# Moving VectorE and GpSimd pieces apart in a hand-ordered gated-attention and feed-forward kernel

## The chip, the cores and the metric

One core of a Trainium2 chip. The metric is the device time of one execution in microseconds, as the median of several runs of the slowest core (there is only one here). TensorE is called PE below, VectorE DVE, ScalarE ACT, GpSimd POOL, and the queue that issues most transfers SP.

## What is computed

A gated linear attention over 768 steps for 32 heads of width 48, whose output goes through a feed-forward layer:

```python
f = 1.0 / (1.0 + np.exp(-f_logit))            # q, k, v, f_logit: (4, 8, 768, 48), fp32
for t in range(S):
    state = f[:, :, t, :, None] * state + np.einsum('bhd,bhe->bhde', k[:, :, t], v[:, :, t])
    y[:, :, t] = np.einsum('bhd,bhde->bhe', q[:, :, t], state)
x = y.transpose(0, 2, 1, 3).reshape(B * S, H * D)      # (3072, 384)
h = x @ w_in                                           # w_in (384, 2048)
g = 0.5 * (h + np.sqrt(h * h + 4.0))
out = g @ w_out                                        # w_out (2048, 384)
```

## The kernel before

The 3072 rows are cut into 12 pairs of two chunks (256 steps each, three pairs to a batch entry). Within a chunk the recurrence is done as matrix products: with the running sum of log f inside the chunk, q is scaled by its negative exponential, k by the positive one, a masked product of q and k gives the part from inside the chunk, and a carried state gives the rest.

The whole kernel is a list of *pieces*. `describe` (L125) defines each piece by name with the engines that may run it; `ORDER` is one long string that lists all 1032 pieces as `name:engine`, with PSUM banks behind `@` for those that take one, and with `TABLE:e` and `TABLE:s` where ACT loads the table for exponentials and logarithms or the one for square roots (six of each). The loop at L567 walks the string and emits piece after piece. Each engine runs its own pieces in the order of the string, and a piece waits until what it reads is there and the buffer that it writes is free. So the string sets everything: the engine of a piece, its place in that engine's queue, and what stands behind it when it waits.

The pieces of pair p, with the lines that the trace shows (L137 and L140 are the helpers for copies and products, so their rows are told apart by the tiles):

- `lf, lq, lk, lv` load f_logit, q, k, v (SP). `wi0` to `wi3` and `wo0` to `wo7` load the weights w_in and w_out in blocks, issued by POOL (L146, L151).
- `ex`, `ln` (ACT, L180, L188) make s, the negative log of f. `ad` adds the two rows of a partition into ss (L194). `hi` and `lo` split ss into two fp16 halves in the tile hl (cast L137, subtraction L203), `cu` sums them along the chunk on PE (L211, L217), `c1` subtracts (L225, tile cm), `ea` and `ep` are the exponentials (ACT, L236), `ge` another small one (L259), `gs` and `gb` small products of it.
- `qm`, `km` make the scaled q and k in the tile qk (products L140, inputs q and ea or k and ep), two each per pair. `vc` casts v to fp16 (tile v16, L137). `tp`, `te` (pairs 0 to 3, PE and copies) or `tx` (pairs 4 to 11, transposing transfers on SP) transpose qk into qkT.
- `sc` (PE, L319), `pm` (DVE, L327, applies the mask while reading PSUM), `kv` (PE, L338), `yt` (PE, L388), `yn` (PE, L397), `sp`, `sa`, `sb` (state update, tiles st and sn), `yc` (copy of y). `xp`, `xe` or `xx` transpose y into xT.
- `m1.p.m` (PE, L436, six matmuls), `sq` (ACT, L445, the square, tile hsq), `rt` (ACT, L450, the root, tile r16, one for two squares), `gt` (DVE, L460, g from PSUM and r), `m2` (PE, L472, four matmuls), `ev` (copy of the output), `st` (store, L493).

Pieces `ad, hi, lo, gs, gb, qm, km, vc`, and `sa, sb` where the state comes from st, read SBUF alone. They may run on DVE or POOL (`hi` and `vc` also on ACT). `pm, gt, c1, sp` and the copies out of PSUM read PSUM and can't run on POOL. `r16` has three buffers: a root waits until the `gt` pieces of three roots earlier have read theirs.

Of the kernel before, what the change touches and what calls it, by code (L numbers as in the profile page):

```python
# [30 lines left out]
tp0.1:T@23 te0.0.0:D te0.1.0:A hi2.0:P te0.0.1:D te0.1.1:A lk2.0:S wi0:P lo2.0:D ea1.00:A sc0.1:T@45 ea1.01:A km1.01:P
sc0.0:T@67 ep1.00:A pm0.11:D lv1.0:S vc0.0:A cu2.0:T@0 pm0.00:D vc0.1:A qm1.01:P pm0.01:D kv0:T@23 ep2.01:A lq2.0:S wi2:P
pm0.10:D ea2.01:A ex3.0:A sa0:D yt0:T@56 km1.00:P c12.0:D ge2:A yn0.1:T ea2.00:A yc0.0:D qm1.00:P ia0.1:T lf5.0:S ep2.00:A
yc0.1:D xp0.0:T@7 ge1:A gb1:P xp0.1:T@4 xe0.0:A wi1:P tp1.0:T@20 ln3.0:A xe0.1:D ex4.0:A ad3.0:D m1.0.1:T@5 te1.1.0:D ln4.0:A
m1.0.0:T@1 te1.0.0:D sq0.1:A ad4.0:P sb0:D sc1.1:T@67 sq0.0:A sc1.0:T@40 pm1.11:D TABLE:s gs2:P lv2.0:S hi3.0:P m1.0.5:T@2
pm1.01:D lo3.0:P pm1.10:D m1.0.4:T@3 rt0.0:A pm1.00:D wi3:P cu3.0:T@7 sq0.5:A gt0.0:D gs1:P sq0.4:A km2.00:P gt0.1:D
m1.0.3:T@0 rt0.2:A c13.0:D km2.01:P lq3.0:S m1.0.2:T@6 sq0.3:A vc1.0:D sq0.2:A gt0.5:D kv1:T@41 lk3.0:S ia1.0:T rt0.1:A
gt0.4:D yt1:T@52 qm2.00:P sa1:D yn1.0:T TABLE:e yc1.0:D qm2.01:P gt0.2:D xp1.0:T@3 yn1.1:T ia1.1:T xe1.0:D ea3.00:A gb2:P
yc1.1:D tp2.0:T@45 wo1:P ep3.00:A sb1:D ep3.01:A xp1.1:T@6 wo3:P lf6.0:S m1.0.6:T@3 te2.1.0:D ea3.01:A ge3:A ex5.0:A
m1.0.7:T@2 te2.0.0:D wo0:P xe1.1:D sq0.6:A sc2.0:T@17 wo2:P lv3.0:S gt0.3:D sc2.1:T@54 ln5.0:A m1.1.3:T@6 pm2.00:D vc2.0:P  # L40
# [5 lines left out]
ep5.01:A c15.0:D m2.0.02:T ep4.01:A c14.0:D ep5.00:A m2.0.12:T gt1.6:D ge5:A ge4:A ex6.0:A lq4.0:S m2.0.03:T vc3.0:P ea4.01:A
m2.1.03:T ep4.00:A ev0.0:D lv4.0:S ea4.00:A xp2.1:T@4 gs4:D xp2.0:T@0 ev1.0:D ln6.0:A tp3.0:T@32 xe2.1:D gb4:D kv3:T@15
xe2.0:D ex7.0:A ad6.0:P lk5.0:S m1.2.3:T@4 sa3:D ea5.01:A te3.0.0:D m1.2.2:T@0 ln7.0:A km4.00:P te3.1.0:D m2.0.13:T lf8.0:S
ea5.00:A ad7.0:P sp3.1:D sq2.3:A sc3.1:T@17 ev0.1:D sc3.0:T@32 sq2.2:A m1.2.0:T@5 km4.01:P pm3.00:D TABLE:s lf9.0:S
m1.2.1:T@6 pm3.10:D qm4.00:P pm3.01:D m2.1.10:T@3 rt2.1:A hi6.0:D m1.2.5:T@1 vc4.0:P sq2.0:A m1.2.4:T@2 gt2.2:D sq2.1:A  # L50
gt2.3:D m2.1.11:T sq2.4:A pm3.11:D km5.00:P m1.2.7:T@0 rt2.0:A qm4.01:D m1.2.6:T@4 km5.01:P sq2.5:A gt2.0:D tx4.0:S m2.1.12:T
rt2.2:A gb5:D lo6.0:P gt2.1:D m2.1.13:T sq2.6:A m2.2.10:T@7 gt2.4:D hi7.0:P tx4.1:S ev1.1:A qm5.01:P gt2.5:D yt3:T@56 sq2.7:A
kv4:T@23 sb3:D rt2.3:A qm5.00:P yn3.1:T yc3.0:D m2.2.00:T@1 yc3.1:D TABLE:e m2.2.01:T lo7.0:P tx5.0:S sp4.0:D cu6.0:T@5
gt2.7:D sa4:P m2.2.11:T ex9.0:A gt2.6:D xp3.0:T@6 tx5.1:S xp3.1:T@2 ep6.01:A cu7.0:T@0 xe3.1:D ex8.0:A xe3.0:D m2.2.02:T
sp4.1:D ge7:A ea7.01:A c16.0:D sc4.1:T@42 ep7.01:A lv5.0:S sc4.0:T@63 pm4.10:D ge6:A ep6.00:A m2.2.03:T lk7.0:S ln8.0:A
pm4.01:D m1.3.0:T@4 lq7.0:S c17.0:D ea6.00:A lk6.0:S m2.2.12:T ad8.0:P pm4.00:D ep7.00:A m2.2.13:T ea6.01:A ev2.0:D sb4:P
ea7.00:A pm4.11:D sc5.0:T@30 ln9.0:A sc5.1:T@65 hi8.0:P pm5.00:D m1.3.1:T@1 gs5:P sq3.0:A vc5.0:P ev2.1:D yt4:T@23 sq3.1:A
pm5.01:D lo8.0:P yn4.0:T TABLE:s m1.3.5:T@7 pm5.11:D ad9.0:P yn4.1:T yc4.0:D m1.3.7:T@0 yc4.1:D rt3.0:A m1.3.4:T@5 qm7.01:P
pm5.10:D xx4:S sq3.5:A kv5:T@23 gt3.0:D km7.00:P yt5:T@63 sq3.4:A gt3.1:D yn5.0:T sq3.7:A lf10.0:S m1.3.3:T@4 sp5.0:D
km6.01:P rt3.2:A lv7.0:S m1.3.2:T@1 sa5:D lq6.0:S hi9.0:P yc5.0:D m1.3.6:T@2 sq3.3:A lv6.0:S km6.00:P gt3.5:D sq3.2:A yn5.1:T  # L60
# [550 lines left out]
```

## Time and profile before

| | |
|---|---|
| median of 3 runs | 199.15 us (198.51 to 201.0) |
| the profiled execution, its own time | 198.22 us |
| its span in the trace | 196.3 us |
| PE busy (matmul) | 169.8 us, 86% |
| ACT busy | 162.3 us, 83% |
| DVE busy | 155.2 us, 79% |
| POOL busy | 86.7 us, 44% |

Busy time is what the trace books between start and end of an instruction; an instruction that waits for something after it has started counts as busy. A row of a timeline gives start, length, engine, line, operation, the tiles written and read, how many instructions are merged in it, and in brackets the idle time of the engine ahead of it with what ended it. Consecutive instructions of an engine overlap by up to a tenth of a microsecond, so starts are a better measure of a step than lengths.

### The profile page before, as it was taken

The page shows a single profiled execution, that of the slowest core. Times are in us where ns is not written, and L with a number is a line of the kernel's source. Part 1 is how long each engine was busy: PE and PEld are TensorE (multiplying, and loading weights), DVE is VectorE, ACT ScalarE, POOL GpSimd, SP SyncE. Part 2 cuts the span into 40 slices and gives each one's busy share as a digit, 9 for nine tenths or more (in the row PEclk, how much of TensorE's full clock was granted, in tenths as well). Part 3 has the DMA queues.
Part 4 walks back from the last instruction along what each step waited for, and adds up shares of the span by engine and source line. Part 5 has one row for each costly group of instructions (what it writes and reads, how often), then busy time and mean ns, then how long its engine had stood idle before and what let it go on. Part 6 is the DMA issues. An engine that isn't in the chain of part 4 may idle for free.

```text
span 196.3 us, 5562 instructions
## 1 busy us (share of the span) xinstructions
PE 169.8 (86%) x2279; PEld 123.3 (63%) x2279; DVE 155.2 (79%) x285; ACT 162.3 (83%) x268; POOL 86.7 (44%) x117
## 2 busy tenths in 40 slices
PE   0248976998699999979999999999999899999990
PEld 0125654785367676867577776677867767767650
DVE  4489779999979999994999959879687559456450
...
GB/s 138 275 261 249 248 251 267 240 217 224 242 135 80 16 136 173 244 183 294 129 227 129 243 292 168 230 146 90 219 170 102 147 80 3 85 106 14 80 83 82
DMA packets 80538, 32.88 MB, mean 167 GB/s; under 512 B 73888, under 2 KB 80496, under 8 KB 80512
## 3 DMA queue, kind: packets, MB, share of 16 engines
...
q0 software_dynamic: 3824, 3.24, 10.3%
...
## 4 chain that ended last, share of the span: by engine, by line
issue 30%; ACT 25%; DVE 20%; PE 15%; DMA 4%; POOL 3%; SPq 1%; POOLq 0%; DVEq 0%; ACTq 0%
DVE g L460 7%; ACT r L450 6%; PE ps L436 6%; ACT hsq L445 4%; DVE pm L327 3%; PE ps L472 3%; ACT ep L236 3%; ACT ea L236 3%; ACT f L180 2%; ACT s L188 2%; DMA q<-in_q_dram 2%; ACT L571 2%; DVE v L137 2%; DMA f<-in_f_logit_dram 1%; POOL sn L140 1%
## 5 line engine op out<-in xcount | busy, mean ns | idle before, releaser
L460 DVE SCALAR_TENSOR_TENSOR g<-ps,r 128x512 f16<-128x512 f32 x96 | 62.2, 684 | 18.7 <-ACT r L450 18.2
L436 PE MATMUL ps<-xT,win 128*128 128x256 f16 x576 | 71.9, 276 | 3.3 <-DMA win<-in_moe_w_in_dram 1.1
L472 PE MATMUL ps<-wout,g 128*128 128x384 f16 x384 | 70.5, 326 | 0.3 <-DVE g L460 0.2
L436 PEld LDWEIGHTS <-win 128*128 128x128 f16 x576 | 55.3, 99 | 14.1 <-DMA xT<-y 2.8
L445 ACT ACTIVATE hsq<-ps 128x512 f16<-128x512 f32 x96 | 54.1, 601 | 11.9 <-PE ps L436 11.6
L450 ACT ACTIVATE r<-hsq 128x1024 f16<-128x1024 f16 x48 | 50.5, 1063 | 4.2 <-DVE g L460 3.4
L472 PEld LDWEIGHTS <-g 128*128 128x128 f16 x384 | 35.9, 98 | 20.8 <-DVE g L460 1.4
L327 DVE TENSOR_TENSOR pm<-ps,mask 128x512 f16<-128x512 f32 x48 | 30.5, 684 | 1.5 <-PE ps L319 1.5
L140 POOL TENSOR_TENSOR qk<-q,ea 128x384 f16<-128x384 f32 (+1 forms) x19 | 18.4, 978 | 13.8 <-DMA q<-in_q_dram 12.6
L140 POOL TENSOR_TENSOR qk<-k,ep 128x384 f16<-128x384 f32 (+1 forms) x20 | 20.1, 1012 | 4.4 <-DMA k<-in_k_dram 4.3
L211 PE MATMUL ps<-hl,tri 128*128 128x384 f16 (+1 forms) x26 | 7.3, 355 | 13.0 <-DVE hl L137 6.3
L194 POOL TENSOR_TENSOR ss<-s 128x384 f32<-128x384 f32 x8 | 8.1, 1009 | 18.2 <-ACT s L188 18.2
L140 POOL TENSOR_TENSOR sn<-st,gs 128x384 f16<-128x384 f32 x5 | 4.1, 829 | 25.4 <-DVE st L364 25.4
L137 DVE CAST y<-ps 128x384 f16<-128x384 f32 x20 | 10.8, 550 | 3.0 <-PE ps L397 2.9
L180 ACT ACTIVATE f<-f 128x768 f32<-128x768 f32 (+1 forms) x13 | 10.3, 795 | 2.6 <-DMA f<-in_f_logit_dram 2.5
L211 PEld LDWEIGHTS <-tri 128*128 128x128 f16 x26 | 2.4, 102 | 14.0 <-issue 7.1
L493 POOL DMA_DIRECT2D out_dram<-os x1 | 0.6, 604 | 22.8 <-DVE os L137 22.8
L188 ACT ACTIVATE s<-f 128x768 f32<-128x768 f32 (+1 forms) x13 | 10.5, 807 | 0.2
L140 DVE TENSOR_TENSOR qk<-q,ea 128x384 f16<-128x384 f32 (+1 forms) x7 | 9.2, 1312 | 1.7 <-issue 1.5
L319 PE MATMUL ps<-qkT 48*64 48x128 f16 x384 | 9.0, 229 | 1.2 <-DVE qkT L137 0.5
L319 PEld LDWEIGHTS <-qkT 48*64 48x64 f16 x384 | 6.4, 112 | 4.9 <-issue 2.8
L137 POOL CAST v<-v 128x768 f16<-128x768 f32 x9 | 8.2, 913 | 2.6 <-PE ps L436 1.5
...
## 6 DMA issues: line engine op xcount, KB each, us to landing
...
```

Of the source, the lines that this page charges most:

```text
L137: eng(e).tensor_copy(out=o, in_=i)
L140: eng(e).tensor_tensor(out=o, in0=a, in1=b, op=ALU.mult)
L180: nc.scalar.activation(out=t, in_=t, func=AF.Exp, scale=-1.0)
L188: nc.scalar.activation(out=T["s", p][:, :, hs], in_=T["f", p][:, hs].rearrange("p h i d -> p i h d"), func=AF.Ln, bias=1.0)
L236: nc.scalar.activation(out=T[nm, p][:, i, hs].rearrange("p h d -> p (h d)"), in_=src_, func=AF.Exp, scale=sgn)
L319: nc.tensor.matmul(out=T["sc", p, i, h][64 * cc:64 * cc + 64, j, :], lhsT=t[r, 1, j, i, :], rhs=t[r, 0, j], start=True, stop=True)
L327: eng(e).tensor_tensor(out=T["pm", p, i, h], in0=T["sc", p, i, h], in1=K["mask"][:, i].unsqueeze(1).broadcast_to([128, 4, 128]), op=ALU.mult)
L436: nc.tensor.matmul(out=T["h", p, m][:, a], lhsT=K["win"][m // 2][:, j, m % 2 * 256 + a * 128:m % 2 * 256 + a * 128 + 128], rhs=T["xT", p][ ...
L445: nc.scalar.activation(out=T["hsq", p, r][:, a], in_=T["h", p, m].rearrange("p a c t -> p (a c t)"), func=AF.Square, scale=1.0)
L450: nc.scalar.activation(out=T["r16", p, r], in_=T["hsq", p, r], func=AF.Sqrt, scale=0.25, bias=1.0)
L460: nc.vector.scalar_tensor_tensor(out=T["g", p][:, 2 * m:2 * m + 2, :].rearrange("p a t -> p (a t)"), in0=T["h", p, m].rearrange("p a c t - ...
L472: nc.tensor.matmul(out=T["o", p, cc], lhsT=T["g", p][:, jn, cc * 128:(cc + 1) * 128], rhs=K["wout"][jn // 2][:, jn % 2, :], start=(jn == 0 ...
```

## The change

Only the string `ORDER` changes. It holds the same 1032 pieces, with the same code, buffers and depths. They stand in another order, many have other PSUM banks, and 70 have another engine: 29 go from DVE to POOL, 20 from POOL to DVE, one from POOL to ACT, nine from DVE to ACT, ten from ACT to DVE, one store from SP to POOL. The pieces that read SBUF alone with two inputs or for a cast were 42 on DVE and 92 on POOL and are 34 and 100.

The diff replaces the string from its first line to its last. One line of each, around the end of pair 1's first layer:

```diff
 ORDER = """
...
-m2.0.10:T@6 rt1.0:A qm3.00:D qm3.01:P m2.0.01:T rt1.2:A gt1.1:D m1.1.7:T@0 lo4.0:P gs3:D lo5.0:D m2.0.11:T sq1.6:A gt1.0:D
...
+rt1.0:A wo6:P m2.0.10:T@3 sq1.4:A gt1.1:D qm3.01:P m2.0.00:T@6 sq1.6:A gt1.0:D m2.0.01:T rt1.2:A km3.01:P m2.0.11:T sq1.7:A
...
```

Four places, as the instructions stand in the built programs. A name is tile, underscore, buffer. The first is DVE from the last y copies of pair 2 to the g of pair 1 (g_962 before, g_960 after); y16 is the y copy, ss the sum, gs a small product, hl the split sum, qk the scaled q and k, ps a PSUM bank. Before:

```order
L137 CAST y16_937<-ps4_885 128x384
L194 TENSOR_TENSOR ss_943<-s_810 128x384
L137 CAST y16_937<-ps1_884 128x384
L460 SCALAR_TENSOR_TENSOR g_962<-ps6_812,r16_939 128x512
L460 SCALAR_TENSOR_TENSOR g_962<-ps0_824,r16_939 128x512
L140 TENSOR_TENSOR qk0_95<-q_596,ea_692 128x4x2x48
L460 SCALAR_TENSOR_TENSOR g_962<-ps7_861,r16_980 128x512
L140 TENSOR_TENSOR gs_999<-ge_754,half_87 128x24
L203 TENSOR_TENSOR hl1_92<-ss_943,hl1_92 128x8x48
L460 SCALAR_TENSOR_TENSOR g_962<-ps5_872,r16_980 128x512
L460 SCALAR_TENSOR_TENSOR g_962<-ps2_945,r16_988 128x512
L460 SCALAR_TENSOR_TENSOR g_962<-ps4_955,r16_988 128x512
```

After:

```order
L137 CAST y16_943<-ps2_889 128x384
L137 CAST y16_943<-ps7_888 128x384
L460 SCALAR_TENSOR_TENSOR g_960<-ps3_873,r16_945 128x512
L460 SCALAR_TENSOR_TENSOR g_960<-ps6_824,r16_945 128x512
L460 SCALAR_TENSOR_TENSOR g_960<-ps1_862,r16_980 128x512
L460 SCALAR_TENSOR_TENSOR g_960<-ps4_813,r16_980 128x512
L460 SCALAR_TENSOR_TENSOR g_960<-ps5_949,r16_1003 128x512
L460 SCALAR_TENSOR_TENSOR g_960<-ps0_936,r16_1003 128x512
```

The ss sum of pair 5, a q product of pair 3, a gs and the subtraction of pair 5 no longer stand between these g; the two y copies and the six g are the same.

The second is POOL in the same stretch, from the eighth block of w_out on (wout7) to the cast of v of pair 3 (v16). Before:

```order
L137 CAST hl1_92<-ss_943 128x8x48
L151 DMA wout7_120<-in_moe_w_out_dram 128x2x384
L151 DMA wout6_119<-in_moe_w_out_dram 128x2x384
L140 TENSOR_TENSOR qk0_95<-q_596,ea_692 128x4x2x48
L203 TENSOR_TENSOR hl0_91<-ss_491,hl0_91 128x8x48
L140 TENSOR_TENSOR qk0_95<-k_629,ep_732 128x4x2x48
L137 CAST v16_1084<-v_789 128x768
```

After:

```order
L151 DMA wout7_120<-in_moe_w_out_dram 128x2x384
L194 TENSOR_TENSOR ss_922<-s_822 128x384
L137 CAST hl1_92<-ss_922 128x8x48
L140 TENSOR_TENSOR qk0_95<-k_668,ep_728 128x4x2x48
L203 TENSOR_TENSOR hl1_92<-ss_922,hl1_92 128x8x48
L151 DMA wout6_119<-in_moe_w_out_dram 128x2x384
L140 TENSOR_TENSOR qk0_95<-q_604,ea_691 128x4x2x48
L140 TENSOR_TENSOR qk0_95<-k_668,ep_728 128x4x2x48
L140 TENSOR_TENSOR qk0_95<-q_604,ea_691 128x4x2x48
L137 CAST v16_1130<-v_835 128x768
```

POOL now makes the ss sum and the subtraction of pair 5 and all four products of pair 3 (tile qk0); the subtraction for pair 4 (hl0_91) has gone to DVE, and the seventh block of w_out (wout6) stands behind four pieces, three of which POOL did not have before.

The third is POOL near the start, from the ss sum of pair 2 to the third issue of w_in (win0, win2, win1 in this order). Before:

```order
L194 TENSOR_TENSOR ss_239<-s_206 128x384
L137 CAST hl0_91<-ss_239 128x8x48
L146 DMA win0_109<-in_moe_w_in_dram 128x3x512
L140 TENSOR_TENSOR qk1_96<-k_149,ep_237 128x4x2x48
L140 TENSOR_TENSOR qk1_96<-q_179,ea_268 128x4x2x48
L146 DMA win2_111<-in_moe_w_in_dram 128x3x512
L140 TENSOR_TENSOR qk1_96<-k_149,ep_237 128x4x2x48
L140 TENSOR_TENSOR qk1_96<-q_179,ea_268 128x4x2x48
L140 TENSOR_TENSOR gb_420<-gs_208,ge_418 128x8
L146 DMA win1_110<-in_moe_w_in_dram 128x3x512
```

After:

```order
L194 TENSOR_TENSOR ss_253<-s_211 128x384
L146 DMA win0_109<-in_moe_w_in_dram 128x3x512
L203 TENSOR_TENSOR hl0_91<-ss_253,hl0_91 128x8x48
L146 DMA win2_111<-in_moe_w_in_dram 128x3x512
L146 DMA win1_110<-in_moe_w_in_dram 128x3x512
L140 TENSOR_TENSOR qk1_96<-k_171,ep_287 128x4x2x48
```

The cast of pair 2 between the ss sum and win0 is gone to DVE; one subtraction (hl0_91) stands between win0 and win2, and win1 follows win2 directly, ahead of the products of pair 1 (qk1), three of which DVE now makes.

The fourth is DVE among the g of pair 2 (g_1330) after the change; ss_1361 belongs to pair 7 and qk2_97 to pair 5:

```order
L460 SCALAR_TENSOR_TENSOR g_1330<-ps7_1211,r16_1299 128x512
L137 CAST y16_1326<-ps5_1266 128x384
L460 SCALAR_TENSOR_TENSOR g_1330<-ps6_1201,r16_1299 128x512
L194 TENSOR_TENSOR ss_1361<-s_1103 128x384
L140 TENSOR_TENSOR qk2_97<-q_1136,ea_1197 128x4x2x48
L460 SCALAR_TENSOR_TENSOR g_1330<-ps1_1319,r16_1352 128x512
L460 SCALAR_TENSOR_TENSOR g_1330<-ps4_1224,r16_1352 128x512
```

The ss sum and the q product are new on DVE there; before, POOL made both.

## Rows read from the trace of the kernel before

**Rows 1.** The page, part 1: busy us, share of span, instructions.

```profile
PE 169.8 (86%) x2279; PEld 123.3 (63%) x2279; DVE 155.2 (79%) x285; ACT 162.3 (83%) x268; POOL 86.7 (44%) x117
```

**Rows 2.** Busy us by stretch; at the end granted clock, DMA share, GB/s.

```profile
22.00:52.00 30.00, 23.87 (x384) 17.73 (x385) 28.32 (x44) 24.93 (x38) 18.92 (x26) 1.00 1.19 242
...
60.00:120.00 60.00, 58.50 (x789) 42.84 (x788) 54.16 (x97) 58.39 (x95) 38.83 (x46) 1.00 0.99 183
120.00:190.00 70.00, 68.47 (x848) 50.34 (x845) 49.55 (x85) 55.76 (x89) 13.51 (x17) 1.00 0.56 110
```

**Rows 3.** DVE by shape: line, operation, tiles, count | busy us, mean ns.

```profile
L140 DVE TENSOR_TENSOR qk<-q,ea 128x384 f16<-128x384 f32 x5 | 8.1, 1617 | 1.5 <-issue 1.5
...
L137 DVE CAST v<-v 128x768 f16<-128x768 f32 x2 | 3.3, 1631 | 0.0
...
L140 DVE TENSOR_TENSOR qk<-k,ep 128x384 f16<-128x384 f32 x3 | 2.1, 686 | 0.0
```

**Rows 4.** Timeline of DVE: start us, length us, line, operation, tiles.

```profile
22.80 0.56 DVE L194 TENSOR_TENSOR ss<-s 128x384 f32<-128x384 f32 x1 [0.43 <-ACT s L188]
...
45.44 4.55 DVE L140 TENSOR_TENSOR qk<-q,ea 128x384 f16<-128x384 f32 x1
49.92 0.68 DVE L460 SCALAR_TENSOR_TENSOR g<-ps,r 128x512 f16<-128x512 f32 x1
...
52.87 0.54 DVE L140 TENSOR_TENSOR qk<-k,ep 128x384 f16<-128x384 f32 x1
```

**Rows 5.** Timeline of POOL beside the long DVE product.

```profile
45.99 1.01 POOL L140 TENSOR_TENSOR qk<-q,ea 128x384 f16<-128x384 f32 x1
46.96 0.91 POOL L203 TENSOR_TENSOR hl<-ss,hl 128x384 f16<-128x384 f32 x1
47.83 0.99 POOL L140 TENSOR_TENSOR qk<-k,ep 128x384 f16<-128x384 f32 x1
48.77 0.81 POOL L137 CAST v<-v 128x768 f16<-128x768 f32 x1
```

**Rows 6.** Timeline of ACT: the root that waited for g.

```profile
51.85 1.06 ACT L450 ACTIVATE r<-hsq 128x1024 f16<-128x1024 f16 x1 [3.41 <-DVE g L460]
```

**Rows 7.** Timeline of PE between 22 and 52 us.

```profile
22.88 2.74 PE L436 MATMUL ps<-xT,win 128*128 128x256 f16 x12
...
29.53 1.48 PE L436 MATMUL ps<-xT,win 128*128 128x256 f16 x12 [1.11 <-DMA win<-in_moe_w_in_dram]
32.42 0.52 PE L338 MATMUL ps<-v,qk 64*128 64x96 f16 x16 [1.41 <-DVE v L137]
...
50.66 0.34 PE L211 MATMUL ps<-hl,tri 128*128 128x384 f16 x1 [2.46 <-DVE g L460]
```

**Rows 8.** Timeline of POOL: first and third issue of w_in.

```profile
14.76 0.95 POOL L146 DMA_DIRECT2D win<-in_moe_w_in_dram  x1
...
21.82 0.79 POOL L146 DMA_DIRECT2D win<-in_moe_w_in_dram  x1
```

**Rows 9.** Timelines: POOL around idle times, then two hl casts on DVE.

```profile
44.01 0.50 POOL L137 CAST hl<-ss 128x384 f16<-128x384 f32 x1 [6.54 <-DVE ss L194]
...
58.82 1.00 POOL L194 TENSOR_TENSOR ss<-s 128x384 f32<-128x384 f32 x1 [9.24 <-ACT s L188]
59.78 1.00 POOL L140 TENSOR_TENSOR qk<-k,ep 128x384 f16<-128x384 f32 x1
...
62.66 0.99 POOL L140 TENSOR_TENSOR qk<-q,ea 128x384 f16<-128x384 f32 x1
...
41.19 0.36 DVE L137 CAST hl<-ss 128x384 f16<-128x384 f32 x1
...
63.03 0.84 DVE L137 CAST hl<-ss 128x384 f16<-128x384 f32 x1
```

More of the change, by code (lines that the diff above doesn't have):

```diff
@@ L31 @@
[L31 to L40, printed above, removed]
@@ L46 @@
[L46 to L55, printed above, removed]
@@ L56 @@
[L56 to L60, printed above, removed]
@@ new lines @@
+ln4.0:A m1.0.0:T@7 te1.0.0:D sq0.1:A ad4.0:P sc1.0:T@04 sq0.0:A sc1.1:T@65 pm1.01:D TABLE:s hi3.0:P m1.0.4:T@2 sb0:D lo3.0:P
+pm1.00:D m1.0.5:T@4 rt0.0:A lv2.0:S pm1.11:D wi3:P cu3.0:T@3 sq0.4:A km2.00:P c13.0:D sq0.5:A gt0.0:D m1.0.3:T@0 gs2:P
+rt0.2:A pm1.10:D gs1:P m1.0.2:T@5 gt0.1:D vc1.0:P lq3.0:S sq0.3:A gt0.5:D sq0.2:A km2.01:P kv1:T@76 gt0.4:D rt0.1:A ia1.0:T
+yt1:T@14 qm2.00:P lk3.0:S sa1:D yn1.0:T TABLE:e yn1.1:T yc1.0:D qm2.01:P yc1.1:D xp1.0:T@2 ia1.1:T gt0.3:D ea3.01:A hi4.0:P
+tp2.0:T@71 ep3.01:A gt0.2:D gb2:P wo2:P ea3.00:A xp1.1:T@4 m1.0.6:T@0 te2.1.0:D ge3:A ep3.00:A lf7.0:S wo0:P ex5.0:A
@@ new lines @@
+yt3:T@05 rt2.1:A sa3:D m1.2.5:T@3 km4.01:P sp3.1:D sq2.0:A yn3.1:T m1.2.1:T@1 yc3.0:D gb4:P gt2.2:D km4.00:P m1.2.6:T@2
+sq2.1:A yc3.1:D m2.1.10:T@0 sq2.5:A gt2.3:D tx4.0:S rt2.0:A m1.2.4:T@7 ad7.0:D m1.2.7:T@5 qm5.00:D sq2.4:A hi7.0:P gt2.1:D
+m2.1.11:T tx4.1:S sq2.7:A sb3:P gt2.0:D cu6.0:T@6 sq2.6:A km5.00:P rt2.2:A m2.1.12:T c16.0:D xp3.0:T@1 lf8.0:S lo7.0:P
+m2.1.13:T rt2.3:A gt2.4:D m2.2.00:T@4 vc4.0:P TABLE:e m2.2.01:T qm5.01:D km5.01:P cu7.0:T@7 ev1.1:D ea6.00:A gt2.5:D
+m2.2.10:T@0 ea6.01:A tx5.0:S c17.0:D m2.2.11:T xe3.0:D ep7.01:A gt2.7:D xp3.1:T@3 ge7:A m2.2.12:T ge6:A ep6.01:A xe3.1:D
@@ new lines @@
+ln11.0:A kv7:T@63 gs7:P sp6.1:D gb7:P yn6.1:T sq5.2:A m2.4.00:T@1 yc6.0:D sb6:P ea9.00:A m1.5.1:T@0 yc6.1:D sq5.3:A ad10.0:P
+sp7.0:D xx6:S m1.5.0:T@2 TABLE:s m2.4.01:T sa7:D gs9:P m2.4.02:T rt5.1:A sp7.1:D st1.01.1:S qm8.00:P m2.4.03:T st2.01.0:S
+sq5.0:A gt5.2:D lk9.0:S m1.5.6:T@7 ev4.0:A gb8:P gt5.3:D km8.00:P lq9.0:S sq5.1:A sc7.0:T@63 sc7.1:T@41 lv8.0:S rt5.0:A
+pm7.00:D m1.5.5:T@5 ad11.0:P pm7.11:D m1.5.4:T@6 sq5.5:A pm7.01:D lq10.0:S m1.6.0:T@1 sq5.4:A pm7.10:D m1.6.2:T@3 sq5.6:A
+gt5.0:D rt5.2:A st3.01.0:S m1.5.7:T@4 gt5.1:D m1.6.1:T@2 hi10.0:D sq5.7:A gt5.4:D lo10.0:P m1.6.5:T@0 rt5.3:A gt5.5:D
@@ new lines @@
+ea10.00:A lk10.0:S ea11.01:A m1.6.6:T@4 pm8.10:D lv10.0:S ep10.00:A pm8.01:D m2.6.10:T@1 ea10.01:A st2.01.1:S ge11:A sq6.6:A
+kv9:T@02 st3.01.1:S sq6.7:A yt8:T@73 sa9:D TABLE:s m2.6.02:T sp9.1:D yn8.0:T m1.7.1:T@0 yc8.0:D rt6.3:A yn8.1:T sb9:D
+m1.7.2:T@2 yc8.1:A gt6.7:D m1.7.0:T@7 vc10.0:P sq7.2:A xx8:S gt6.6:D m1.7.5:T@3 sq7.1:A km10.00:P sq7.0:A m1.7.4:T@5 tx9.0:S
+rt7.0:A km10.01:D m2.6.11:T qm10.01:P m1.7.6:T@4 sq7.5:A gt7.1:D qm10.00:P sq7.4:A m2.6.03:T tx9.1:S gt7.0:D rt7.2:A
+m1.7.3:T@0 m2.6.12:T sq7.3:A gt7.5:D tx10.1:S m1.7.7:T@7 rt7.1:A ev6.0:D m2.7.00:T@3 gt7.4:D sq7.7:A m1.8.3:T@6 gs10:D
@@ new lines @@
+st5.01.0:S m1.8.5:T@7 rt8.3:A sa10:P st7.01.0:S m2.8.00:T@3 sq8.5:A gb11:P gt8.7:D qm11.01:P m2.8.01:T rt8.2:A gt8.6:D
+m1.9.0:T@5 tx11.1:S m1.9.1:T@2 gt8.5:D yn10.0:T gt8.4:D yn10.1:T m1.9.4:T@7 yc10.1:A sp10.1:D sq9.0:A m1.9.5:T@0 yc10.0:D
+sq9.1:A m1.9.2:T@6 sb10:D xx10:S sq9.4:A gs11:D m2.8.02:T sq9.5:A m1.9.3:T@1 rt9.2:A st5.01.1:S m2.8.10:T@4 tx11.0:S sq9.2:A
+gt9.5:D m2.8.03:T sq9.3:A rt9.0:A m1.9.6:T@0 ev8.0:D m2.8.11:T gt9.4:D rt9.1:A gt9.1:D m1.9.7:T@3 gt9.0:D sq9.6:A m2.8.12:T
+sq9.7:A gt9.3:D m2.8.13:T rt9.3:A gt9.2:D sc11.1:T@72 sc11.0:T@51 pm11.11:D m2.9.10:T@6 pm11.01:D m1.10.4:T@2 ev8.1:D
@@ new lines @@
+m1.10.2:T@1 sq10.4:A pm11.00:D m2.9.11:T pm11.10:D m1.10.5:T@4 gt9.7:D gt9.6:D kv11:T@57 sq10.5:A yt11:T@37 sp11.0:D rt10.2:A
+m2.9.12:T sa11:D m2.9.00:T@0 sq10.2:A m1.10.3:T@5 yn11.1:T yn11.0:T sq10.3:A m2.9.13:T yc11.1:D yc11.0:A m2.9.01:T rt10.1:A
+xx11:S m1.10.0:T@7 gt10.3:D m1.10.1:T@3 sq10.0:A st8.01.0:S ev9.1:D m1.10.7:T@5 sq10.1:A st6.01.1:S gt10.4:D m2.9.02:T
+rt10.0:A st6.01.0:S m2.9.03:T sq10.7:A gt10.1:D m1.10.6:T@6 gt10.0:D m1.11.3:T@2 sq10.6:A gt10.2:D m1.11.0:T@3 ev9.0:A
+st9.01.0:S m2.10.00:T@7 sq11.0:A st8.01.1:S m1.11.1:T@0 rt10.3:A st9.01.1:S m1.11.2:T@1 st7.01.1:S gt10.6:D m2.10.01:T
@@ new lines @@
+sq11.2:A gt10.5:D m1.11.6:T@6 sq11.1:A gt10.7:D rt11.0:A m2.10.10:T@4 m1.11.5:T@5 sq11.3:A gt11.1:D m2.10.02:T sq11.6:A
+gt11.0:D rt11.1:A m1.11.7:T@0 m1.11.4:T@3 sq11.7:A gt11.2:D m2.10.11:T sq11.4:A gt11.3:D m2.10.12:T sq11.5:A rt11.3:A
+m2.10.13:T m2.11.00:T@1 rt11.2:A gt11.7:D m2.11.10:T@2 ev10.1:A gt11.5:D m2.11.01:T gt11.4:D m2.10.03:T gt11.6:D m2.11.11:T
+ev10.0:A m2.11.02:T st10.01.0:S m2.11.03:T st10.01.1:S m2.11.12:T ev11.01:D ev11.00:A m2.11.13:T st11.0.0:S st11.0.1:P
+ev11.11:D ev11.10:D st11.1.0:S st11.1.1:P
```

90 lines of the change are left out of this document (40 added, 50 removed).

## The prediction

> **What bounds the kernel now.** I read three views: the page's shares, a table by stretches, and the timelines around the longest holes. The shares [rows 1] name three engines close together, PE 169.8, ACT 162.3 and DVE 155.2 us of a 196.3 us span, and so settle nothing. The table by stretches [rows 2] does. From 60 to 120 us PE is busy 58.50 and ACT 58.39 of 60 us: both are full, and DVE's 54.16 has room. From 120 to 190 us PE alone is full (68.47 of 70). From 22 to 52 us neither is: PE 23.87 and ACT 24.93 of 30, while DVE has 28.32. So DVE sets the pace there and nowhere else. The granted clock is 1.00 in every stretch; it is no part of this.
>
> What fills DVE in that stretch is partly waiting that is booked as busy. By shape [rows 3], the q product of 128x384 takes 1617 ns as a mean of five on DVE, and the same shape for k takes 686; the fp32 cast of v takes 1631. All read SBUF alone, twice or for a cast. One of the five is the outlier [rows 4]: it runs from 45.44 for 4.55 us, and the next g begins at 49.92. Over those microseconds POOL runs four instructions back to back, from 45.99 to 49.58 [rows 5]; DVE ends 0.41 us after the last of them. A clean one takes 0.54, the last row of [rows 4], so some 4.0 us of the 4.55 are waiting. It is on the path: r, the square root on ACT, waits 3.41 us for the g behind it and starts at 51.85 [rows 6], and PE then sits 2.46 us until 50.66 [rows 7].
>
> **The change, part by part.** It moves no work away: all pieces stay. I counted the pieces that have two SBUF inputs or an SBUF cast: DVE had 42 and has 34, POOL 92 and now 100. What matters is where the 34 stand. On DVE, between the xT copies of pair 0 and the last g of pair 1 (22 to 56 us before), there were eight: an ss sum, the cast of v, a cast and a subtraction for hl, another ss, the two products of pair 3 and a gs. Afterwards there is one, the subtraction for pair 4. From the first of them at 22.80 to the last at 52.87 [rows 4] their start-to-start steps sum to 8.7 us: 4.48 for the long product, 1.96 for the v cast, 2.15 for five others of full width, 0.09 for gs. With the added one at 0.47 the net is 8.2. So DVE falls from 28.3 to some 20 us of work in that stretch and stops being its bound.
>
> *What bounds it next.* ACT: it has 24.93 us of work in these 30 [rows 2], and the order gives it nearly the same squares, roots, exponentials and the same three table loads there. So this stretch can shrink by 5.07 us at most. 3.41 of these hang on the one product and go with it. The remaining 1.66 are short waits for first-layer matmuls; two things that delayed those matmuls go as well: the third weight block was issued on POOL at 21.82 [rows 8], and PE waited 1.11 us for it until 29.53 [rows 7]; four products stood ahead of it, now one subtraction; and PE waited 1.41 us for the v cast until 32.42 [rows 7], which now waits for no g of DVE's. ACT was busy during most of both, so I book half of the 1.66. Part one: **-4.2** (bounds: -2.4, if the product's place is taken by another 1 us wait, and -5.1).
>
> *The start.* The first layer begins at 22.88 [rows 7], 8.1 us after its weights were issued at 14.76 [rows 8]; the third block's gap, 21.82 to 29.53, is 7.7, and that row names the transfer, so I take the first layer to wait for its weights too. Ahead of that first issue POOL had eight pieces and still has eight, but the hl cast of pair 2 that stood last, some 0.5 us with its wait, is on DVE now, and the subtraction for pair 2, which POOL takes over, stands behind the issue. I estimate **-0.9**; bounds 0 (POOL's ss sum that precedes it waits for ACT's logarithm, which may be no earlier) and -2.
>
> *What POOL pays.* A product costs it 1.01 and a subtraction 0.91 [rows 5] where DVE takes 0.55. Seven of the eight pieces at 0.45 to 1.01 each (gs is small), less the subtraction of pair 4, are some 5 us more for it between 22 and 52. It was busy 18.92 of 30 there [rows 2], and later it stands idle 9.24 us before 58.82 [rows 9]; the work fits into idle time, cost 0. If that cover were gone, 5 us would go onto the transposes of pair 3 at most.
>
> *After 52 us.* PE and ACT have the same pieces in about the same interleaving. PE's idle time from 60 to 190 is 3.03 us [rows 2], part of it waits for transposed y; the new order puts a little more PE work between the last y product of a pair and the first use of its transpose in six of the eight pairs that are transposed by DMA. But ACT, full from 60 to 120, must follow a PE that comes earlier. I take 0, bounds +2 and -3.
>
> *What contention is left.* The 34 pieces still meet POOL at times. An ordinary meeting costs a few tenths: the hl cast took 0.36 at 41.19, when POOL was idle, and 0.84 at 63.03, beside POOL products that ran from 59.78 on [rows 9]. I add **+0.4** for one on the path.
>
> Sum, against the profiled execution's own 198.22 us: 198.22 - 4.2 - 0.9 + 0.4 = **193.5**. The median of the runs shown, 199.15, is 0.9 above that execution; I leave that in the range.
>
> **The skill against the rows.** The rows show a DVE product that waited through four POOL instructions [rows 4, 5]. The Trainium skill, "SBUF — State Buffer", section on its two separate sides, says that the shared pair of ports is an exclusive lock, held for one instruction, and that a VectorE instruction with two SBUF inputs contends with a GpSimd one that reads SBUF. That it contends, the trace confirms; that one instruction is the wait, it does not: by the rule the product would have taken at most 0.55 + 1.01 = 1.56 us, about 3 us less than measured, and part one would be worth about -1.6. The measurement decides: the rule could only change a price that the row settles, and the sum goes by the row. The "GPSIMD Engine Reference", section on engine selection, speaks against the change: two-input elementwise work is about twice as slow there. The rows agree (1.01 against 0.54), but the sum pays for this only if POOL's idle time runs out.
>
> **The rivals.**
> *Eaten later (0.24).* The 4 to 5 us arrive at 52 us, and ACT, full to 120 us, gives part of them back: one more us of its work stands ahead of the middle stages by the new order, and two or three meetings with POOL of 0.5 us fall on the path. Gain left 0.5 to 3: 195.2 to 197.7, up to 198.5 against the median, taken as 196.5. For it: 58.39 of 60. Against it: ACT gets its early work earlier by the same amount.
> *Deeper (0.16).* The start gives 2, the first stretch all 5.07, PE's waits for transposes 2 more: 198.22 - 9 = 189.2.
> *The separation does not hold on the chip (inside the first rival).* The order separates by planned times; if real ones drift, the long wait returns elsewhere. The row at 63.03 says that a usual meeting costs 0.5, not 4.
> *Slower (0.05).* The place is DVE's ss sum and q product of pairs 7 and 5, which stand in the middle of the g of pair 2, next to an unbroken row of nine POOL pieces, some 6.4 us by their prices. If DVE arrives when that row starts and starves as at 45.44, it loses up to 6 us, and with it the g behind it, PE and ACT. It must lose over 4.7 in all to undo the gain and about 8.7 to be 2% slower: the full 6 here and 4 at a second such place give 203.5. Against: beside POOL's long row of before the cast at 63.03 waited 0.5 [rows 9].
>
> **How the numbers follow.** Forecast (191 to 195.2) 0.55, eaten 0.24, deeper 0.16, slower or even 0.05. The likeliest is 193.5. The range 189.5 to 198.5 leaves out part of the deeper case and the slow one. About 2% is what a measurement of this kernel can tell from no change; that line is at 195.2 us. Faster: 0.55 + 0.16, less 0.01 for the edge, 0.70. Same 0.26, slower 0.04.
>
> **What would show it.** Right: no DVE product over 2 us in the changed profile; DVE's busy time lower by about 9 us; the root ahead of the third table load of the exponentials starting near 47 instead of 51.85 us with no wait for g of over 1 us; first layer at 22 us. Wrong: that root at 47 us and yet a span of 195 (eaten later: then ACT or PE shows new holes after 60 us); a long DVE piece beside a row of POOL ones at another place; or PE waiting for wout, whose seventh block now stands behind four POOL pieces of pair 5 and 3.

## The result and the profile after

The changed kernel takes 188.43 us (median of 4 runs, 188.21 to 189.48) beside 198.83 us (197.42 to 201.0) for the kernel before on the same chip: ratio 0.951, 95% interval 0.944 to 0.958. Here and below medians are over all runs, while ratios leave out runs more than 1.5% above the fastest of the same kernel. Its profiled execution took 188.35 us with a span of 186.6; the one of before took 198.22 with 196.3. The gain between the two profiled ones is 9.9 us. The forecast was 4.7 us of gain and 193.5 us; 188.4 lies 1.1 us below the range of 189.5 to 198.5, next to the time of the rival called "deeper" (189.2).

The page after, part 1 (busy us, share of the span, instructions), to be held against [rows 1]:

```profile
PE 167.3 (90%) x2279; PEld 123.0 (66%) x2279; DVE 145.1 (78%) x277; ACT 161.1 (86%) x268; POOL 90.2 (48%) x126
```

DVE's busy time is 10.1 us lower, with eight instructions fewer of 285. By stretch (window, its length, busy us of PE, weight loads, DVE, ACT and POOL, granted clock, DMA share, GB/s), against [rows 2]:

```profile
22.00:52.00 30.00, 27.67 (x455) 20.14 (x453) 25.59 (x47) 29.51 (x47) 22.63 (x32) 1.00 1.17 233
60.00:120.00 60.00, 59.36 (x856) 43.77 (x854) 53.75 (x95) 58.85 (x100) 36.01 (x45) 1.00 0.99 190
120.00:180.00 60.00, 59.04 (x659) 43.90 (x658) 42.05 (x72) 46.76 (x72) 9.63 (x11) 1.00 0.53 113
```

From 22 to 52 us ACT is now busy 29.51 of 30; it was 24.93. DVE no longer bounds that stretch. DVE by shape after, against [rows 3]:

```profile
L140 DVE TENSOR_TENSOR qk<-k,ep 128x384 f16<-128x384 f32 x4 | 3.1, 781 | 0.0
L140 DVE TENSOR_TENSOR qk<-q,ea 128x384 f16<-128x384 f32 x5 | 2.9, 582 | 0.0
L137 DVE CAST v<-v 128x768 f16<-128x768 f32 x2 | 1.5, 754 | 0.0
```

The q product is down from a mean of 1617 ns to 582 and the cast of v from 1631 to 754; the k product is up from 686 to 781. Three timelines after show the path (start, length, engine, line, operation, tiles, idle time before and what ended it). PE in the first layer, against [rows 7]:

```profile
21.07 1.49 PE L436 MATMUL ps<-xT,win 128*128 128x256 f16 x12
...
24.21 1.48 PE L436 MATMUL ps<-xT,win 128*128 128x256 f16 x12 [1.05 <-DMA win<-in_moe_w_in_dram]
...
26.95 1.48 PE L436 MATMUL ps<-xT,win 128*128 128x256 f16 x12 [0.74 <-DMA win<-in_moe_w_in_dram]
```

PE's waits for w_in have not gone: they are 1.05 and 0.74 us, where there was one of 1.11 [rows 7]. ACT around the last root of pair 1, against [rows 6]:

```profile
44.12 0.64 ACT L445 ACTIVATE hsq<-ps 128x512 f16<-128x512 f32 x1
44.79 1.06 ACT L450 ACTIVATE r<-hsq 128x1024 f16<-128x1024 f16 x1
```

DVE in the same place:

```profile
42.39 1.29 DVE L460 SCALAR_TENSOR_TENSOR g<-ps,r 128x512 f16<-128x512 f32 x2 [0.63 <-ACT r L450]
44.30 1.29 DVE L460 SCALAR_TENSOR_TENSOR g<-ps,r 128x512 f16<-128x512 f32 x2 [0.63 <-ACT r L450]
```

The root had waited 3.41 us for DVE's g; now DVE waits for ACT's root, and the root starts 7.06 us earlier. The first layer begins 1.81 us earlier (22.88 to 21.07). The last output issue starts at 182.87 instead of 192.46 us, 9.59 us earlier. So the start gave 1.8, the stretch up to that root another 5.25, and what follows it another 2.5.

### The profile page after: what moved, and what is told of

The parts are those of the page before. It is cut to its first block, busy times and chain, and to the rows that moved or that the text cites. A ratio compares the mean times of both kernels' runs of the same rounds, so it can differ in the third digit from the quotient of the medians.

```text
span 186.6 us, 5571 instructions
## 1 busy us (share of the span) xinstructions
PE 167.3 (90%) x2279; PEld 123.0 (66%) x2279; DVE 145.1 (78%) x277; ACT 161.1 (86%) x268; POOL 90.2 (48%) x126
## 4 chain that ended last, share of the span: by engine, by line
PE 48%; issue 22%; DMA 15%; POOL 6%; SPq 5%; ACT 1%; POOLq 0%
PE ps L436 20%; PE ps L472 18%; DMA q<-in_q_dram 7%; POOL qk L140 4%; DMA qkT<-qk 3%; DMA f<-in_f_logit_dram 3%; SPq L173 3%; DMA k<-in_k_dram 3%; SPq L278 2%; PE ps L319 2%; PE ps L388 2%; PE ps L338 2%; PE ps L211 1%; PE ps L397 1%; PE ps L295 1%
## 5 line engine op out<-in xcount | busy, mean ns | idle before, releaser
L140 POOL TENSOR_TENSOR qk<-k,ep 128x384 f16<-128x384 f32 (+1 forms) x19 | 19.3, 1019 | 18.7 <-PE ps L388 10.5
L140 POOL TENSOR_TENSOR qk<-q,ea 128x384 f16<-128x384 f32 (+1 forms) x19 | 18.7, 990 | 4.0 <-ACT ea L236 2.2
L493 POOL DMA_DIRECT2D out_dram<-os x2 | 1.1, 575 | 39.0 <-ACT os L135 38.4
L137 POOL CAST v<-v 128x768 f16<-128x768 f32 x9 | 7.8, 862 | 14.2 <-DMA v<-in_v_dram 8.8
L194 POOL TENSOR_TENSOR ss<-s 128x384 f32<-128x384 f32 (+1 forms) x10 | 9.9, 991 | 6.0 <-ACT s L188 5.9
L137 DVE COPY os<-ps 128x384 f32<-128x384 f32 (+1 forms) x17 | 8.5, 513 | 2.9 <-PE ps L472 2.9
L203 POOL TENSOR_TENSOR hl<-ss,hl 128x384 f16<-128x384 f32 (+1 forms) x11 | 9.7, 881 | 2.0 <-DVE hl L137 1.8
L137 DVE CAST y<-ps 128x384 f16<-128x384 f32 x15 | 8.1, 551 | 2.2 <-PE ps L397 2.0
L135 ACT CAST y<-ps 128x384 f16<-128x384 f32 x9 | 4.2, 475 | 5.2 <-PE ps L397 3.8
```

The costliest lines, as they stand in the source:

```text
L137: eng(e).tensor_copy(out=o, in_=i)
L140: eng(e).tensor_tensor(out=o, in0=a, in1=b, op=ALU.mult)
L194: eng(e).tensor_tensor(out=T["ss", p][:, hs], in0=T["s", p][:, 0, hs], in1=T["s", p][:, 1, hs], op=ALU.add)
```

## The experiments

A word of the string is a piece with its engine letter: D is DVE, P POOL, S SP, T PE. Every experiment computes all of the reference. Its string is three lines shorter than that of the kernels before and after, so its rows show line numbers lower by three: L137 is the product helper there (L140 before and after), and L134 the helper for copies. Times go with the ratio to the kernel before, run on the same chip.

**One product on POOL, the rest as before.**

```diff
-qm3.00:D
+qm3.00:P
```

> The kernel before with one change: the q product of pair 3 that took 4.55 us on DVE (qm3.00) goes to POOL, at the same place of the string. Theory A (DVE's waits behind POOL made the loss): the root that waited 3.41 us for it no longer waits, time lower by 3 to 3.5 us, about 195.4. Theory B (the new order made the gain, by weights and inputs that come earlier and more PE work ahead of each wait): within 1 us of before, since ACT or PE gives it back.

Measured: a median of 200.05 us, from runs of 197.42, 198.18, 201.91 and 205.54, beside 197.77 to 204.02 for the kernel before: no gain that can be told. The product's 4.55 us are gone, but the next DVE piece that reads SBUF takes its place. POOL, then DVE:

```profile
45.38 0.71 POOL L148 DMA_DIRECT2D wout<-in_moe_w_out_dram  x1
46.12 1.96 POOL L137 TENSOR_TENSOR qk<-q,ea 128x384 f16<-128x384 f32 x2
48.03 0.91 POOL L200 TENSOR_TENSOR hl<-ss,hl 128x384 f16<-128x384 f32 x1
48.90 0.98 POOL L137 TENSOR_TENSOR qk<-k,ep 128x384 f16<-128x384 f32 x1
49.84 0.81 POOL L134 CAST v<-v 128x768 f16<-128x768 f32 x1
```

```profile
47.28 3.41 DVE L137 TENSOR_TENSOR gs<-ge,half 128x24 f32<-128x24 f32 x1
```

A product of 24 elements a row waits until the POOL row ends at 50.65 us. The root starts at 51.85 us, as before:

```profile
51.85 1.06 ACT L447 ACTIVATE r<-hsq 128x1024 f16<-128x1024 f16 x1 [3.29 <-DVE g L457]
```

The price does not belong to the product; it belongs to the row on POOL and fell here on the next SBUF piece of DVE.

**Eight pieces of the first stretch on POOL, one back, in the order of before.**

```diff
-ad3.0:D vc1.0:D hi4.0:D ad5.0:D qm3.00:D gs3:D lo5.0:D km3.00:D lo4.0:P
+ad3.0:P vc1.0:P hi4.0:P ad5.0:P qm3.00:P gs3:P lo5.0:P km3.00:P lo4.0:D
```

> The kernel before with only the engine letters of nine pieces as in the changed kernel: the eight of 22 to 56 us go to POOL, the subtraction for pair 4 to DVE; the order of the string stays. A: the gain up to 52 us that does not come from the start, 4 to 5 us, about 194. B: 1 us or less more than with the one product alone.

Measured: 192.96 us, ratio 0.968 (0.961 to 0.975). The root starts 4.48 us earlier:

```profile
47.37 1.06 ACT L447 ACTIVATE r<-hsq 128x1024 f16<-128x1024 f16 x1
```

The last output issue is 4.66 us earlier: what was won stays. Which of the seven pieces besides the product were needed was not tried one by one.

**All engines of after in the order of before, and the order of after with the engines of before.** The first has the 70 changed letters on the old string, the second the old letters on the new string.

> The order of before with the engines of after for all 70 pieces that changed engine. A: most of the gain, 6 to 10 us, 189 to 193. B: 2 to 4 us (what the one product gives), 195 to 197, since POOL and DVE pieces meet at other places of the old order.

> The order of after with the engines of before for those 70 pieces. A: DVE's pieces meet POOL again and the time goes back to 195 to 199. B: the order keeps most of the gain, 189 to 192.

Measured: 199.24 us, ratio 0.9985 (0.995 to 1.002), and 198.4 us, ratio 0.994 (0.990 to 0.999). Neither half is worth anything that counts. With the engines alone the first layer begins 1.70 us later (24.58), and between 80 and 160 us PE loses 4.14 us to waits, one of them for a state that POOL now makes:

```profile
85.28 0.33 PE L394 MATMUL ps<-sn,qkT 128*128 128x96 f16 x4 [1.46 <-POOL sn L137]
```

With the order alone a DVE product again meets a POOL row behind a weight issue and takes 2.65 us, and PE waits for the g behind it:

```profile
41.55 2.65 DVE L137 TENSOR_TENSOR qk<-k,ep 128x384 f16<-128x384 f32 x1
```

```profile
44.85 0.81 PE L469 MATMUL ps<-wout,g 128*128 128x384 f16 x4 [1.73 <-DVE g L457]
```

**Two weight issues earlier, nothing else.** In all three long waits so far (4.55, 3.41 and 2.65 us) POOL had issued a block of w_out right ahead of its row. Here they stand elsewhere; the product stays on DVE.

```diff
-... wo4:P ... hi5.0:P ... wo7:P ... wo6:P ... qm3.01:P
+... wo4:P wo7:P wo6:P ... hi5.0:P ... qm3.01:P
```

> Before, with the last two weight issues of POOL (wo7, wo6) moved up to stand right behind wo4; the long product qm3.00 stays on DVE and now meets the row qm3.01, lo4.0, km3.01, vc3.0 without an issue ahead of it. In the three cases seen so far in which a DVE piece waited for two to four POOL pieces (4.55, 3.41, 2.65 us), POOL had issued wo6 right before the row. Theory 'the issue opens the row' (DVE loses its turn only while POOL comes out of an issue): qm3.00 takes at most 0.55 + 1.0 = 1.6 us, the root rt1.3 starts near 49 instead of 51.85 us, and the time falls by 2 to 3 us, to about 196.5. Theory 'a row without a gap is enough': qm3.00 or the gs3 behind it still takes 3 to 4.5 us, the root stays near 51.9, the time within 0.5 us of before.

Measured: 196.02 us (193.71 to 198.26; before on that chip 198.84 to 202.32), ratio 0.974 (0.963 to 0.985), which rests on two runs: a gain, but of uncertain size. DVE, then POOL:

```profile
45.47 0.79 DVE L137 TENSOR_TENSOR qk<-q,ea 128x384 f16<-128x384 f32 x1
...
47.19 0.84 DVE L137 TENSOR_TENSOR gs<-ge,half 128x24 f32<-128x24 f32 x1
47.95 1.22 DVE L200 TENSOR_TENSOR hl<-ss,hl 128x384 f16<-128x384 f32 x1
```

```profile
44.85 1.00 POOL L137 TENSOR_TENSOR qk<-q,ea 128x384 f16<-128x384 f32 x1
45.81 1.22 POOL L200 TENSOR_TENSOR hl<-ss,hl 128x384 f16<-128x384 f32 x1
```

The row on POOL is the same four pieces without a gap, yet the product takes 0.79 us instead of 4.55: it waits for the one POOL piece that runs, goes next, and POOL's subtraction is longer by 0.3 us (1.22 against 0.91 in [rows 5]). The root starts at 49.86 us, 2.0 earlier. The profiled execution was the slowest of the four, 198.26 us, and by its end it has lost the 2 us again: its last output issue is at 192.59 us, 0.1 later than before. One of the waits that cost it is 1.32 us of PE for a transposed q and k, until 76.75 us. So its trace shows the shorter wait, not what that is worth in time.

**The product back on DVE in the kernel after, then also without the issue right ahead.**

```diff
-... gt1.1:D ... qm3.00:P
+... qm3.00:D gt1.1:D ...
```

> After, with the one product qm3.00 given back to DVE at its old place among the g of pair 1. Theory 'the meeting is the price': it meets wo6, qm3.01 and km3.01 on POOL, takes 2.5 to 3.5 us, the root rt1.3 moves from 44.8 to 47 or later and the time rises by 2 to 3 us to about 191. Theory 'other pieces of the order make the gain': it takes 0.6 to 1.6 us, hidden by ACT, and the time stays within 0.7 us of after's 188.4.

In the second, besides:

```diff
-wo7:P ... lo5.0:P ... wo6:P ... qm3.01:P
+wo7:P wo6:P ... lo5.0:P ... qm3.01:P
```

> After with the product qm3.00 back on DVE (as in e6_product_back, where it took 2.65 us behind the issue wo6 and two POOL products), and now wo6 moved up to stand right behind wo7, so that no issue stands ahead of that row of POOL. Theory 'an issue ahead of the row makes DVE wait for the whole row': qm3.00 takes at most 1.6 us, probably 0.6 to 1.0. Theory 'any row without a gap does': again 2 to 2.7 us. The time is 188.2 to 189.3 by both, since ACT hides either.

Measured: 189.29 us, ratio 0.947 (0.939 to 0.956), and 189.99 us, ratio 0.951 (0.945 to 0.957). In the first, DVE:

```profile
41.50 2.65 DVE L137 TENSOR_TENSOR qk<-q,ea 128x384 f16<-128x384 f32 x1
```

and POOL beside it:

```profile
40.99 0.76 POOL L148 DMA_DIRECT2D wout<-in_moe_w_out_dram  x1
41.77 1.01 POOL L137 TENSOR_TENSOR qk<-q,ea 128x384 f16<-128x384 f32 x1
42.73 1.00 POOL L137 TENSOR_TENSOR qk<-k,ep 128x384 f16<-128x384 f32 x1
```

In the second, DVE, then POOL:

```profile
45.24 1.26 DVE L137 TENSOR_TENSOR qk<-q,ea 128x384 f16<-128x384 f32 x1
```

```profile
45.09 0.99 POOL L137 TENSOR_TENSOR qk<-q,ea 128x384 f16<-128x384 f32 x1
46.05 1.31 POOL L137 TENSOR_TENSOR qk<-k,ep 128x384 f16<-128x384 f32 x1
```

With the issue right ahead, both POOL products go first; with the issue moved up, only the running one. POOL's row still follows on the issues without a gap, but they now end at 41.66 us, four pieces ahead of the one that DVE meets. The time of the first cannot be told from after's. In its trace, of the 2.1 us of waiting, the root behind it comes 1.3 us later by its distance from the first layer, and the end 1.1. The rise of 2 to 3 us that one theory expected is not there; about half of the wait is hidden. (The profiled execution of the second had a granted clock of 0.93 between 22 and 47 us; only these rows of it are read here.)

**The same question the other way round.** One load of q, issued by POOL instead of SP, stands ahead of a POOL row near 105 us, where no wait of DVE's had been over 1.32 us.

```diff
-lq10.0:S ... qm8.01:P ... km9.01:D ... sb7:P ... qm9.01:D qm9.00:P ... hi11.0:P
+lq10.0:P qm8.01:P ... km9.01:D ... sb7:P ... qm9.01:D qm9.00:P ... hi11.0:P
```

> After with one load of q, that of pair 10, issued by POOL instead of SP, right ahead of its product qm8.01 (near 105 us), where DVE's product km9.01 meets POOL's row qm8.01, sb7, qm9.00; in after it waited for one of the three and took 1.32 us. The same question the other way round. Theory 'an issue ahead of the row': km9.01 arrives during the issue or the first product behind it and waits for all of the row, 2.5 to 4.5 us. Theory 'no effect of the issue': 0.55 to 1.6 us. The time within 1 us of after's 188.4 by the second, 1 to 3 us longer by the first.

Measured: 190.9 us, ratio 0.956 (0.950 to 0.962); the interval overlaps that of after. POOL, then DVE:

```profile
106.89 0.94 POOL L170 DMA_DIRECT2D q<-in_q_dram  x1
107.85 1.01 POOL L137 TENSOR_TENSOR qk<-q,ea 128x384 f16<-128x384 f32 x1
108.80 0.83 POOL L137 TENSOR_TENSOR sn<-st,gb 128x384 f16<-128x384 f32 x1
109.59 1.00 POOL L137 TENSOR_TENSOR qk<-q,ea 128x384 f16<-128x384 f32 x1
110.53 0.84 POOL L134 CAST hl<-ss 128x384 f16<-128x384 f32 x1
```

```profile
107.00 0.55 DVE L137 TENSOR_TENSOR qk<-k,ep 128x384 f16<-128x384 f32 x1
...
108.06 2.95 DVE L137 TENSOR_TENSOR qk<-q,ea 128x384 f16<-128x384 f32 x1
```

The product named in the expectation, km9.01, runs within the issue and is clean (0.55). The next one, qm9.01, which took 0.58 in the kernel after, comes 0.2 us into the row and waits for three POOL pieces: 2.95 us. The nearest like case in after is km9.01, which came 0.1 us into a row without an issue and waited for one piece (1.32 us). In the trace the pieces behind it come 1.6 us later than those ahead of it, compared with after.

**The start.** The order of after up to the first table load of the roots, then the order with eight pieces (five PSUM banks chosen anew).

> The kernel with eight pieces on POOL (e2_eight, 193.0 us), with its order up to the first table load of the square roots (the first 124 words, up to about 22 us) taken from after; behind it the order of e2_eight. Theory 'the terms add': the first layer begins at 21.1 instead of 22.85 us and the end comes 1.8 us earlier: 191.2. Theory 'the start is hidden again by ACT or PE behind it': the first layer earlier, the time still 192.5 to 193.

And of that start only the third weight issue, in the kernel with eight pieces:

```diff
-wi2:P ... km1.00:P ... qm1.00:P ... gb1:P ... wi1:P
+wi2:P wi1:P ... km1.00:P ... qm1.00:P ... gb1:P
```

> The kernel with eight pieces on POOL (e2_eight, 193.0 us), with the issue of the third weight block (wi1) moved up right behind wi2, past four POOL pieces; nothing else of the start of after. The prediction's theory 'the first layer waits for weights': PE's wait for win near 28.4 to 29.5 us goes, and the end comes 0.5 to 1 us earlier, 192.0 to 192.5. Theory 'the start is set by the products and sums of pair 0': the first layer begins at 22.85 as before (or later, since the products of pair 1 on POOL come 0.8 us later), the wait for win shrinks, and ACT makes nothing of it: 192.7 to 193.3.

Measured: 191.34 us, ratio 0.959 (0.953 to 0.964), and 193.62 us, ratio 0.970 (0.964 to 0.975), against 0.968 for the eight pieces alone. The whole start is worth some 1.7 us (first layer at 20.99 us); the third weight issue alone is worth nothing. It comes 2.9 us earlier, the first layer still begins at 22.77, and PE's waits for w_in only shrink from 1.01 us to 0.84:

```profile
26.30 1.48 PE L433 MATMUL ps<-xT,win 128*128 128x256 f16 x12 [0.20 <-DMA win<-in_moe_w_in_dram]
28.93 1.49 PE L433 MATMUL ps<-xT,win 128*128 128x256 f16 x12 [0.64 <-DMA win<-in_moe_w_in_dram]
```

Nor does the first layer wait for its first block: in the trace of the kernel before that lands at 21.89 us, 1.0 us before the first layer begins. What its start follows in the traces is the chain of pair 0. On DVE, before, the subtraction of pair 1 waits for a cast of POOL's and stands ahead of four products of pair 0, the last of which is this:

```profile
10.75 0.94 DVE L203 TENSOR_TENSOR hl<-ss,hl 128x384 f16<-128x384 f32 x1 [1.53 <-POOL hl L137]
13.30 1.15 DVE L140 TENSOR_TENSOR qk<-k,ep 128x192 f16<-128x192 f32 x1
15.60 1.56 DVE L203 TENSOR_TENSOR hl<-ss,hl 128x384 f16<-128x384 f32 x1
17.09 0.68 DVE L327 TENSOR_TENSOR pm<-ps,mask 128x512 f16<-128x512 f32 x1
```

After, POOL makes the subtractions of pairs 1 and 2 (the 10.75 and 15.60 us rows). The last product of pair 0 on DVE, and the first mask:

```profile
12.33 0.35 DVE L140 TENSOR_TENSOR qk<-k,ep 128x192 f16<-128x192 f32 x1
15.15 0.69 DVE L327 TENSOR_TENSOR pm<-ps,mask 128x512 f16<-128x512 f32 x1 [0.47 <-PE ps L319]
```

That product ends 1.77 us earlier (12.68 against 14.45), the scores that the first mask reads are ready 1.77 earlier (15.11 against 16.88), the mask starts 1.94 earlier and the first layer 1.81. The subtraction of pair 2 at 15.60, which met POOL behind the issue of w_in [rows 8], held the mask back by some 0.2 us only. So the cause lies ahead of these products, and which change there gives the 1.77 us was not tried alone; the wait of 1.53 us that stood ahead of them is one that is gone.

**The late part.** The kernel with eight pieces up to the third table load of the exponentials, and everything behind it as in after (nine banks chosen anew).

> The kernel with eight pieces on POOL (e2_eight, 193.0 us) up to the third table load of the exponentials (about 48 us); all that follows in the order and with the engines of after (nine of its PSUM banks had to be chosen anew). Theory 'the late order is worth the 2.5 to 3 us by which after gains beyond 52 us': 190.0 to 190.5. Theory 'nothing after 52 us, as predicted; the late gain comes out of the early part': 192.5 to 193.

Measured: 191.18 us, ratio 0.957 (0.952 to 0.962): 1.8 us less than the eight pieces alone; in the trace the last output issue is 2.0 us earlier. PE is the bound there, and its idle time from 80 to 160 us tells where it comes from. The sums of that stretch (length, busy us of PE, weight loads, DVE, ACT, POOL) for the eight pieces and for this kernel:

```profile
sum 80.00, PE 77.20 PEld 57.30 DVE 66.01 ACT 71.28 POOL 32.98; mean PE 38.60 PEld 28.65 DVE 33.01 ACT 35.64 POOL 16.49
```

```profile
sum 80.00, PE 79.10 PEld 59.26 DVE 67.16 ACT 71.15 POOL 34.63; mean PE 39.55 PEld 29.63 DVE 33.58 ACT 35.58 POOL 17.32
```

Idle 2.80 us against 0.90, a difference of 1.9. Before and after have 2.77 and 0.96:

```profile
sum 80.00, PE 77.23 PEld 57.73 DVE 65.20 ACT 72.16 POOL 37.03; mean PE 38.62 PEld 28.86 DVE 32.60 ACT 36.08 POOL 18.52
```

```profile
sum 80.00, PE 79.04 PEld 58.74 DVE 66.91 ACT 70.57 POOL 31.72; mean PE 39.52 PEld 29.37 DVE 33.46 ACT 35.29 POOL 15.86
```

Before, the waits were 0.99 us for a copy of y (at 86.00), 1.07 for a transposed y (at 152.98) and 0.39 for an exponential (at 126.06). Of these, after has only one of 0.90 for a transposed y (at 143.96).

**The last of these waits.** In the kernel after, one PE piece, the state product of pair 9, moves ahead of two others, so that its y is transposed earlier.

```diff
-sc10.1:T@03 pm10.01:D m2.7.13:T pm10.10:D m1.8.7:T@5 pm10.11:D yn9.1:T
+sc10.1:T@03 yn9.1:T pm10.01:D m2.7.13:T pm10.10:D m1.8.7:T@5 pm10.11:D
```

> After with one word moved: the state product yn9.1 on PE stands 1.3 us earlier, ahead of two other PE pieces, so that y of pair 9 is copied and transposed earlier. After's largest wait of PE beyond 80 us is the 0.90 us for this transpose at 143.96. Theory 'beyond 80 us PE is the bound, and each of its waits for a transpose is worth its length' (by which the late order gains 1.9 us): the wait goes and the time falls by 0.7 to 1.0 us, to about 187.5. Theory 'a wait of PE there is given back behind it': the time stays within 0.3 us of after's 188.4.

Measured: 187.65 us (six runs, 186.64 to 188.33), ratio 0.939 (0.935 to 0.944). PE has no wait left there; its idle time between 120 and 160 us falls to 0.07:

```profile
120.00:160.00 40.00, 39.93 (x542) 30.14 (x535) 31.45 (x55) 32.37 (x49) 9.68 (x11) 1.00 0.66 136
```

In the trace its distance to after shrinks by 1.06 us across that place: 1.04 later at the first-layer piece ahead of it, 0.02 earlier at the one behind it. This is one pair of traces; the medians are 0.8 us apart, from separate sets of runs. The kernel is the best of the kernels run.

## Why the prediction was wrong

The sign and, for the first stretch, the mechanism were right: most of what the prediction named as proof is there. No DVE product takes over 2 us (the longest is 1.32), DVE's busy time is 10.1 us lower, the root before the table load starts at 44.79 us without a wait, PE does not wait for w_out. The two pieces of DVE that the "slower" rival put beside POOL's long row ran clean (0.55 us each at 58.55 and 59.01 us). The sum failed in all four of its terms, all to the same side, and most of all in the term that it put at nothing.

- **The first stretch, -4.2.** 5.25 us were measured from the first layer to the root in the trace of after, 4.4 with eight pieces alone. 5.25 is a little more than the 5.07 that I took as the most that ACT's work allowed; I had booked half of the short waits. And one step in it was wrong: "3.41 of these hang on the one product and go with it". With the product alone gone, the root starts at 51.85 us as before. I did name that bound, "the product's place is taken by another 1 us wait", and priced it at 1; the heir waited 3.2. Nor did PE's wait for w_in go: one of 1.11 us became two, of 1.05 and 0.74.
- **The start, -0.9.** 1.8 was measured, and the step under it was wrong. I read the 8.1 us from the weight issue to the first layer as the transfer, since a second gap of 7.7 us was one. The first block had landed 1.0 us before it was used, and the third block's issue moved alone gives nothing. In the traces the first layer follows the chain of pair 0, whose last product comes 1.77 us earlier after the change; I did not follow that chain.
- **After 52 us, 0.** This is the step that failed most. Some 2.5 us were measured behind the root, 2.0 with the late part alone. The prediction had the pieces of it: PE alone full there, 3.03 us of idle time [rows 2], the waits for transposed y, and an order that puts more PE work in front of them. It then set the price to 0 because ACT, full from 60 to 120 us, must follow. But ACT follows a PE that comes earlier by coming earlier itself, and PE's idle time from 80 to 160 us fell by 1.9 us, nearly what the late part gave. The last experiment shows for one wait that it is worth its length (1.06 us in the trace for a wait of 0.90).
- **Contention left, +0.4.** Not there. What DVE's SBUF pieces take over their clean lengths (the shortest of their kind in any trace), summed over the trace, falls from 12.4 to 3.4 us, and no meeting stands on the path to the root.

The parts add up: in the traces the eight pieces give 4.7, the start 2.3 and the late part 2.0 us at the end of the program, together 9.0 of the 9.6. Each figure is from one trace. By the interval of their ratio the eight pieces give more, 5.0 to 7.9 us; the kernel before scatters from 197.4 to 204 us over its runs, and why it scatters more than the others stays open.

What the row of four POOL pieces had been read as, a product that starves, was a special case. The Trainium skill, "SBUF — State Buffer", section on its two separate sides, gives a lock for one instruction. The prediction set this aside for the row's 4.55 us. The traces have both: with no issue ahead of the row, or one four pieces ahead, the product waited for one POOL piece (0.79, 1.32 and 1.26 us); with one right ahead, DVE waited for two to four (2.65, 2.65, 2.95, 3.41, 4.55). By the rule alone the long waits are not to be had.
